# Expert tiles two pairs earlier, and summary copies ahead of loads, in a fused attention and expert kernel

## The chip, the cores and the metric

One core of a Trainium2 chip. The metric is the device time of one launch in microseconds (us), median of several runs; lower is better. Five engines work side by side, each through its own instructions in order: TensorE (matmuls and transposes; PE in the profile), VectorE (DVE), ScalarE (ACT), GpSimd (POOL), and SyncE (SP), which here only starts transfers. The *clock* in the tables is the share of TensorE's full clock that the profile says was granted.

## The reference, cut to what matters

```python
# attention, 4 batches x 8 heads x 768 x 64: a window of 16 positions around the query,
# plus one summary key (max) and one summary value (mean) for each block of 32
k_sum = k.reshape(B, H, nb, 32, D).max(axis=3);  v_sum = v.reshape(B, H, nb, 32, D).mean(axis=3)
... softmax over [window scores, summary scores + log(32)] ...
x = attn_out.transpose(0, 2, 1, 3).reshape(3072, 512)
# mixture of 8 experts: each token goes to one
logits = x @ w_gate + modality_bias[modality_id];  e_idx = argmax(logits)
for e in range(8):
    out[e_idx == e] = gate[e_idx == e] * (relu(x[e_idx == e] @ w1[e]) @ w2[e])   # F = 1024
```

## The kernel before

Sixteen *pairs* (batch and two heads, numbered 0 to 15; four pairs make a batch) go through attention in a software pipeline. When a batch's four pairs are done, it is *routed*: logits, expert, and the row of each token in a table `xs` in DRAM, sorted by expert. GpSimd *scatters* the batch's tokens there in six indirect transfers, two ticks of the schedule apart. An *expert tile* is 256 consecutive rows of `xs`: loaded (`xr`), transposed (`px`), multiplied by `w1` (`ph`), and by `w2` (`pmo`). Tiles come in lists: two after batch 0, four after batch 1, two after batch 2, and the rest at the end. A tile's steps are cut into up to seven *units*, and a string per pair says in which of its six slots how many are put into TensorE's stream.

The load of a tile's rows reads `xs`, so it may start only after the scatters of its batch. The weights of the first two tiles are guessed and loaded early; the tile itself then issues its weight load under a condition ("only if the guess was wrong") into the same buffers.

```python
UNITS = {9: "000111", 10: "101111", 11: "111111", 12: "101111", ...}   # pair: units in slots 0 to 5
ENLIST = (7, 10, 14)                                                     # pairs at whose end a list is taken up

def weights(lst, j, i):                       # GpSimd, of tile i
    e = nc.gpsimd.value_load(li[0:1, j, 2:3]); go = nc.gpsimd.value_load(li[0:1, j, 3:4])
    load_weights(i % NWB, e, cond=go > 0)     # skipped if go is 0
...
for n in range(np_):                          # pairs
    scores(n, 1);  tick(...);  pump(u[0])     # tick: routing steps and one scatter; pump: expert units
    keys(n + 2)                               # transposes, copies of kv
    ... features, route ...
    load(n + 4)                               # three loads issued by GpSimd
    weights_ahead(n)                          # a guessed weight load, GpSimd
    tick(...);  pump(u[1])
    values(n, 0)
    tick(...)
    summaries(n + 2)                          # VectorE reductions, then GpSimd's copy kv<-ks
    tick(...);  pump(u[2])
    queries(n + 2);  tick(...);  pump(u[3])
    blocks(n + 1);  ... scores(n + 1, 0);  tick(...);  pump(u[4])     # blocks: value transposes (pv)
    ... features ...;  values(n, 1);  tick(...)
    if n in ENLIST: scatter(NC); enlist(lists[b - 1])
    pump(u[5])
```

The softmax here doesn't subtract the row's maximum and nothing guards it: scores larger than these inputs give would overflow.

## Time and profile before

| | before |
|---|---|
| time, median of 3 | 233.79 us |
| profiled span, mean TensorE clock | 228.3 us, 0.903 |
| TensorE busy | 184.0 us (81 %) |
| VectorE, ScalarE, GpSimd busy | 122.8, 119.4, 124.9 us |
| transposes of tiles 0, 1 and 2 start at | 80.2, 94.9, 110.8 us |
| routing of batches 0, 1 and 2 starts at | 41.0, 68.4, 117.1 us |

The profiled execution took 230.08 us, 3.7 us less than the median; spans and times are therefore not to be mixed. TensorE fills the second half of the span, so work moved off it there comes off the time; in the first half it waits for its helpers. The wanted gain is in that first half: fill its holes with expert work from the second. The lines of the profile stand in the prediction.

### The profile page before, as it was taken

How to read it: one execution, taken by the hardware profiler on the slowest of the kernel's cores; microseconds unless marked ns; L12 is line 12 of the kernel's file. 1: busy time of each engine (PE TensorE's matmuls, PEld its weight loads, DVE VectorE, ACT ScalarE, POOL GpSimd, SP SyncE). 2: the span in 40 equal slices, each digit the busy share in tenths (PEclk: the TensorE clock that was granted, in tenths of full speed). 3: DMA queues.
4: the chain of work that ended last, by engine and by line, in shares of the span. 5: the costliest groups of instructions: out<-in, count | busy, mean ns of one | idle time of the engine just before them, and what ended most of it. 6: DMA issues, size and time to landing. Idle time of an engine off the chain costs nothing. (4 is left out here: it accounts for less than half of the span.)

```text
span 228.3 us, 6765 instructions
## 1 busy us (share of the span) xinstructions
PE 184.0 (81%) x2720; PEld 131.5 (58%) x2720; DVE 122.8 (54%) x352; ACT 119.4 (52%) x207; POOL 124.9 (55%) x198
## 2 busy tenths in 40 slices
PE   0676797869696549999789999999959899999900
PEld 0464575667465536766577667576626667766500
DVE  6369979699958994655449763534870111101000
ACT  2586568576854441867457675462424255554410
POOL 8459529738889180498531575311574757372220
PEclk9999589967977575999999999999997999999985
DMA  5979929999999999139950123241121434312100
GB/s 76 136 106 139 188 44 143 187 205 172 203 221 153 227 172 160 37 88 207 200 198 3 70 100 136 81 143 47 69 103 56 157 118 141 112 51 83 52 19 0
DMA packets 20090, 27.44 MB, mean 120 GB/s; under 512 B 2876, under 2 KB 16468, under 8 KB 20052
## 3 DMA queue, kind: packets, MB, share of 16 engines
q0 software_dynamic: 17424, 24.40, 52.8%
q1 hardware_dynamic: 2628, 2.54, 4.0%
q8 instruction: 23, 0.38, 0.7%
q14 instruction: 15, 0.12, 0.2%
HBM read 85.46 MB, written 10.44 MB: 420 GB/s over the span
## 5 line engine op out<-in xcount | busy, mean ns | idle before, releaser
L530 PE MATMUL ph<-xg,w1b 128*128 128x256 f16 x416 | 53.8, 285 | 6.6 <-DVE at L516 3.8
L530 PEld LDWEIGHTS <-w1b 128*128 128x128 f16 x416 | 40.4, 101 | 14.9 <-issue 7.0
L542 PE MATMUL pmo<-w2b,hT 128*128 128x512 f16 x208 | 48.5, 379 | 0.0
L548 POOL DMA_INDIRECT out_dram<-ot,at x26 | 25.9, 997 | 32.8 <-ACT ot L547 22.3
L292 ACT ACTIVATE pT<-pss 128x384 f16<-128x384 f32 x64 | 28.0, 495 | 23.5 <-PE pss L287 23.4
L533 ACT ACTIVATE hT<-ph 128x512 f16<-128x512 f32 x52 | 30.6, 602 | 17.2 <-PE ph L530 16.7
L547 ACT ACTIVATE ot<-pmo,xr 128x512 f32<-128x512 f32 x26 | 17.9, 688 | 27.7 <-PE pmo L542 18.0
L351 POOL DMA_INDIRECT xs<-xb,posi x24 | 24.9, 1040 | 13.1 <-issue 5.3
L542 PEld LDWEIGHTS <-hT 128*128 128x128 f16 x208 | 19.2, 98 | 20.6 <-ACT hT L533 1.4
L238 ACT COPY kv<-pk 128x768 f16<-128x768 f16 x32 | 24.3, 810 | 8.1 <-PE pk L237 7.8
L513 DVE COPY xg<-px 128x1024 f16<-128x1024 f16 x13 | 8.9, 686 | 34.0 <-PE px L511 34.0
L270 PE MATMUL pv<-ident,kv 128*128 128x128 f16 x192 | 16.0, 244 | 4.0 <-POOL kv L251 4.0
L318 DVE TENSOR_TENSOR xb<-po,rec 128x384 f16<-128x384 f32 x32 | 17.8, 557 | 1.0
L241 POOL COPY kv<-kv 128x352 f16<-128x352 f16 x16 | 7.9, 493 | 18.7 <-ACT kv L238 18.5
L270 PEld LDWEIGHTS <-kv 128*128 128x128 f16 x192 | 13.5, 110 | 5.7 <-POOL kv L251 4.4
L248 DVE TENSOR_REDUCE ks<-kv 128x24 f16<-128x768 f16 x16 | 15.1, 944 | 2.2 <-ACT kv L238 2.2
L250 DVE TENSOR_REDUCE ks<-kv 128x24 f16<-128x768 f16 x16 | 15.1, 943 | 0.8 <-ACT kv L238 0.8
L294 DVE TENSOR_TENSOR pT<-pT,bmask 96x768 f16<-96x768 f16 x14 | 8.5, 604 | 13.2 <-ACT pT L292 13.2
L330 DVE COPY xT<-pt 128x768 f16<-128x768 f16 x16 | 8.9, 555 | 12.0 <-PE pt L327 11.8
L271 DVE COPY vb<-pv 120x768 f16<-120x768 f16 x20 | 10.7, 551 | 7.4 <-PE pv L270 7.4
L261 ACT COPY qT<-pq 128x768 f16<-128x768 f16 x16 | 12.9, 809 | 3.0 <-PE pq L259 2.9
L287 PEld LDWEIGHTS <-kv 64*128 64x128 f16 x384 | 8.4, 101 | 10.4 <-issue 8.9
(127 smaller groups left out, 280.7 us busy)
## 6 DMA issues: line engine op xcount, KB each, us to landing
w1b<-in_moe_w_dram POOLq DMA_DIRECT2D x13, 1024.0 KB
w2b<-in_moe_w_dram POOLq DMA_DIRECT2D x13, 1024.0 KB
kn<-in_k_dram POOLq DMA_DIRECT2D x16, 192.0 KB
vn<-in_v_dram POOLq DMA_DIRECT2D x16, 192.0 KB
qn<-in_q_dram POOLq DMA_DIRECT2D x16, 192.0 KB
xr<-xs SPq DMA_DIRECT2D x8, 272.0 KB, 7.1
w1b<-in_moe_w_dram POOLq DMA_DIRECT2D x4, 512.0 KB
w2b<-in_moe_w_dram POOLq DMA_DIRECT2D x4, 512.0 KB
```

The costliest lines, as they stand in the source:

```text
L238: nc.scalar.copy(kv[:, i, :, 0:64].rearrange("p t (s c) -> p t s c", c=C8), bass.AP(pk.tensor, pk.offset, [pk.ap[0], [8, NT], [1, 8], [P8, ...
L248: nc.vector.reduce_max(ks[:, 0], kv[:, 0, :, 0:64].rearrange("p t (g s) -> p t g s", g=2), axis=AX.X)
L250: nc.vector.reduce_sum(ks[:, 1], kv[:, 1, :, 0:64].rearrange("p t (g s) -> p t g s", g=2), axis=AX.X)
L270: nc.tensor.transpose(pv[:, tl, :], kv[:, 1, 6 * half + tl, :], ident)
L292: nc.scalar.activation(pT[:, h], pss[h], AF.Exp, scale=SCALE)
L318: nc.vector.tensor_tensor(xo, po[:, :, :, 0:D], rec.unsqueeze(3).to_broadcast([128, 2, 3, D]), op=ALU.mult)
L351: apart("xs", nc.gpsimd.indirect_dma_start(out=xs[:, :], out_offset=bass.IndirectOffsetOnAxis(ap=posi[:, c:c + 1], axis=0), in_=xb[:, c, : ...
L530: nc.tensor.matmul(ph[:, f, :], w1[:, c, ts(2 * f2 + f, 128)], xg[:, c, :], start=(c == 0), stop=(c == NCD - 1))
L533: nc.scalar.activation(hT[:, 2 * f2:2 * f2 + 2, :], ph, AF.Relu)
L542: nc.tensor.matmul(po, hT[:, f, ts(s2, 128)], w2[:, f, :], start=(f == 0), stop=(f == NF - 1))
L547: nc.scalar.activation(ot, po, AF.Copy, scale=gt)
L548: apart("out", nc.gpsimd.indirect_dma_start(out=out[:, :], out_offset=bass.IndirectOffsetOnAxis(ap=at[:, s2:s2 + 1], axis=0), in_=ot[:], i ...
```

## The change

Its intent: (a) GpSimd's summary copy of a pair goes ahead of that pair's loads in GpSimd's queue, so that the value transposes don't wait for it; (b) start-up memsets go from VectorE to GpSimd; (c) the mask is added by matmul in seven instead of nine pairs; (d) expert units start in pair 7 instead of 9, three a pair at first; (e) for that, routing of batch 0 runs faster, the first list is taken up after pair 6, and the guessed weights are loaded by pair 8. The diff is cut: it leaves out where the other memsets move to, and one empty step fewer in the start-up work.

```diff
-    NMASK = 9
+    NMASK = 7
-        nc.vector.memset(kv[:, :, 0, 64:80], 0.0)          # and four more, three times
+        nc.gpsimd.memset(kv[:, :, 0, 64:80], 0.0)
-    UNITS = {9: "000111", 10: "101111", 11: "111111", 12: "101111", 13: "111111", 14: "111111", 15: "101111"}
-    ENLIST = (7, 10, 14)
+    UNITS = {7: "000111", 8: "001110", 9: "010101", 10: "010101",
+             11: "111110", 12: "101111", 13: "111110", 14: "101111", 15: "101110"}
+    ENLIST = (6, 10, 14)
-        for p in {n + 2: (n,) for n in range(8)}.get(n, ()):
+        for p in {2: (0,), 3: (1,), 4: (2,), 5: (3,), 6: (4,), 7: (5,), 8: (6, 7)}.get(n, ()):
+    T = (1, 2, 2, 2)                                       # routing steps a tick, by batch
...
+        tick(T[b])
+        pump(u[1])
+        values(n, 0)
+        tick(T[b])
+        if n + 2 < np_:
+            summaries(n + 2)
         if n + 4 < np_:
             load(n + 4)
         weights_ahead(n)
-        tick(2 if n >= 8 else 1)
-        pump(u[1])
-        values(n, 0)
-        tick(2 if n >= 8 else 1)
-        if n + 2 < np_:
-            summaries(n + 2)
```

More of the change, by code (lines that the diff above doesn't have):

```diff
@@ L102, in borders @@
         kv, vb = kvs[i], vbs[i]
-        nc.vector.memset(kv[:, :, 0, 64:80], 0.0)
-        nc.vector.memset(kv[:, :, NT - 1, 80:96], 0.0)
-        nc.vector.memset(kv[:, :, :, KR:128], 0.0)
-        nc.vector.memset(vb[0:WK, :, :, D:D + 1], 1.0)
-        nc.vector.memset(vb[WK:KR, :, :, D:D + 1], 32.0)
-    borders(0)
+        nc.gpsimd.memset(kv[:, :, 0, 64:80], 0.0)
+        nc.gpsimd.memset(kv[:, :, NT - 1, 80:96], 0.0)
+        nc.gpsimd.memset(kv[:, :, :, KR:128], 0.0)
+        nc.gpsimd.memset(vb[0:WK, :, :, D:D + 1], 1.0)
+        nc.gpsimd.memset(vb[WK:KR, :, :, D:D + 1], 32.0)
     tok = const.tile([128, NJ], I32, name="tok")
     nc.gpsimd.iota(tok, pattern=[[128, NJ]], base=0, channel_multiplier=1)
+    for i in range(NK):
+        borders(i)
     midc = const.tile([NJ, 128], mybir.dt.int64, name="midc")
@@ L161 @@
     guess = const.tile([128, NWB], I32, name="guess")
+    nc.gpsimd.memset(exl, -1.0)
+    nc.gpsimd.memset(done, 0.0)
+    nc.gpsimd.memset(ones, 1.0)
     def early_constants():
@@ L166, in early_constants @@
         nc.vector.reduce_max(g1, mb0, axis=AX.X)
-        nc.vector.memset(exl, -1.0)
         yield
@@ L171, in early_constants @@
         nc.vector.tensor_tensor(g2, mb0, g1.unsqueeze(2).to_broadcast([128, 2, E]), op=ALU.is_ge)
-        nc.vector.memset(done, 0.0)
         nc.vector.tensor_tensor(g2, g2, erev[:, None, :].to_broadcast([128, 2, E]), op=ALU.mult)
@@ L175, in early_constants @@
         nc.vector.reduce_max(g1, g2, axis=AX.X)
-        nc.vector.memset(ones, 1.0)
         nc.vector.tensor_tensor(exl[:, 0:1], g1[:, 0:1], g1[:, 1:2], op=ALU.max)
@@ L203, in later_constants @@
         nc.vector.tensor_copy(mh, midc.bitcast(I32)[:, 0::2])
-        for _ in range(4):
+        for _ in range(3):
             yield
@@ L625 @@
     load(2)
-    borders(1)
     queries(0)
@@ L632 @@
     load(3)
-    borders(2)
     queries(1)
@@ L648 @@
             side.append(route(b - 1))
+        tick(T[b])
+        pump(u[1])
+        values(n, 0)
+        tick(T[b])
+        if n + 2 < np_:
+            summaries(n + 2)
         if n + 4 < np_:
@@ L651 @@
         weights_ahead(n)
-        tick(2 if n >= 8 else 1)
-        pump(u[1])
-        values(n, 0)
-        tick(2 if n >= 8 else 1)
-        if n + 2 < np_:
-            summaries(n + 2)
-        tick(2 if n >= 8 else 1)
+        tick(T[b])
         pump(u[2])
@@ L661 @@
             queries(n + 2)
-        tick(2 if n >= 8 else 1)
+        tick(T[b])
         pump(u[3])
@@ L665 @@
             blocks(n + 1)
-            tick(2 if n >= 8 else 1)
+            tick(T[b])
             scores(n + 1, 0)
-        tick(2 if n >= 8 else 1)
+        tick(T[b])
         pump(u[4])
@@ L671 @@
             features(n - 1)
-        tick(2 if n >= 8 else 1)
+        tick(T[b])
         values(n, 1)
-        tick(2 if n >= 8 else 1)
+        tick(T[b])
         if n in ENLIST:
```

## The prediction

> **What bounds the kernel now.** I read the page's busy slices first, then the stretches by stage, the waits of the stretch where TensorE is not full, and last the timeline around the first expert tile. The kernel has 16 attention pairs (batch and pair of heads, numbered 0 to 15); the expert tiles of the routed tokens are fed into TensorE's stream in small units (a transpose step, four steps of the first matmul, two of the second), from pair 9 on.
>
> ```profile
> PE   0676797869696549999789999999959899999900
> DVE  6369979699958994655449763534870111101000
> PEclk9999589967977575999999999999997999999985
> DMA  5979929999999999139950123241121434312100
> ```
>
> One digit is 5.7 us. TensorE is full only from slice 16 on (about 91 us). Before that it has gaps, the granted clock falls below full, and VectorE and the DMA engines are near nine tenths. The stretches say it in numbers (columns: length, TensorE, its weight loads, VectorE, ScalarE, GpSimd busy, clock, DMA share, GB/s):
>
> ```profile
> 0.00:42.00 42.00, 28.38 (x651) 21.14 (x652) 31.26 (x96) 26.47 (x44) 27.17 (x52) 0.92 0.82 121
> 42.00:77.00 35.00, 26.18 (x589) 20.48 (x588) 29.38 (x84) 19.99 (x37) 27.12 (x43) 0.77 1.11 195
> 77.00:94.00 17.00, 13.22 (x220) 10.65 (x221) 11.81 (x34) 7.56 (x14) 4.81 (x10) 0.67 0.96 154
> 94.00:157.00 63.00, 60.96 (x853) 41.97 (x851) 36.33 (x96) 38.82 (x70) 33.08 (x51) 1.00 0.41 114
> 157.00:218.00 61.00, 55.28 (x421) 37.30 (x419) 14.02 (x43) 26.61 (x44) 31.86 (x44) 0.97 0.26 94
> ```
>
> From 94 to 157 us TensorE is busy 61.0 of 63 us: it is the bound. From 42 to 77 us (pairs 4 to 8) VectorE is busy 29.4 of 35 us and GpSimd 27.1, TensorE 26.2 at a clock of 0.77: the two helpers set the pace. What TensorE waited for between 17 and 93 us (total, times, longest):
>
> ```profile
> PE pv L270 <- POOL kv L251: 4.0, 3, 2.2
> PE ph L530 <- DVE at L516: 3.8, 1, 3.8
> PE pc L412 <- DVE tot L408: 2.7, 1, 2.7
> PE pr L386 <- DVE oh L378: 2.0, 2, 1.3
> ```
>
> The change aims at the first line (summary copies) and the second (first expert tile). The timeline there (start, length):
>
> ```profile
> 60.21 0.75 POOL L224 DMA_DIRECT2D w1b<-in_moe_w_dram  x1
> 62.30 0.71 POOL L251 COPY kv<-ks 128x576 f16<-128x576 f16 x1
> 63.07 0.84 PE L270 MATMUL pv<-ident,kv 128*128 128x128 f16 x12 [2.17 <-POOL kv L251]
> 65.82 0.98 POOL L351 DMA_INDIRECT xs<-xb,posi  x1 [0.30 <-issue]
> ...
> 69.90 1.58 SPq L488 DMA_DIRECT2D xr<-xs  x2
> ...
> 80.20 1.03 PE L511 MATMUL px<-ident,xr 128*128 128x128 f16 x8
> 86.12 1.87 PE L530 MATMUL ph<-xg,w1b 128*128 128x256 f16 x8 [3.78 <-DVE at L516]
> ```
>
> The summary copy stands behind three loads and a weight load, and TensorE waits 2.17 us for it. The sixth row scatter goes out at 65.82; the load of the tile's rows is issued at 69.90, lands 7.9 us later (about 77.8, from the DMA view), and the tile's transposes run at 80.20. So in this kernel the rows were there 2.4 us before they were used. That margin matters below.
>
> **What the Trainium skill says.** "TensorE: Matmul & The Clock Gate", Part 1: the array falls to half rate after an idle window of about 3.4 us and needs one busy window to come back; the trace agrees, 16 key transposes take 0.53 us at full clock and 0.85 us in the 0.5 stretches. The same page's specifications call GpSimd's queue "strict FIFO" of depth 8: so a copy ahead of loads is early, and loads behind a copy wait for whatever the copy waits for; 62.30 above is that rule. "GPSIMD Engine Reference", 4: GpSimd's cores write the descriptors of its own DMAs; here each load issue holds it 0.65 us and each scatter about 1.0 us (1.3 apart). "DMA: Bandwidth & Descriptors", Anatomy of one DMA: about 2 us fixed per transfer; the scatter above took 4.1 us until its reader could start, with the engines busy.
>
> **The change, part by part.**
> (a) Copies ahead of loads: takes away at most the 4.0 us of waits and, since they set off a half-clock stretch at 64 to 67 us, about 1.5 us more. But VectorE was saturated from 44 to 64 us, and ScalarE has only about 0.9 us of slack around the wait at 37 us, so I count 2.5 us. The cost: loads, weight loads and scatters now stand behind VectorE's reductions.
> (b) Memsets: VectorE loses three times (0.07 + 0.07 + 0.14 + 0.08 + 0.08) and 0.08 + 0.07 + 0.17, 1.8 us in all as listed, some overlapped; it is near full from 14 to 30 us, so about 0.5 us of it counts. GpSimd gets 18 memsets; its known ones last 0.10 us, an iota of 128x128 0.23, so I estimate 2 to 3 us, into the 2.87 us that it waits at 5.8 us. Even.
> (c) Bias in two pairs fewer: 8 matmuls of 128x384 off TensorE at 0.21 us apart, 1.7 us; four multiplies of 0.604 us onto VectorE (2.4 us), one 0.55 us copy off it onto ScalarE at 0.80.
> (d) Expert units: 36 before the last batch's routing in both (3, 5, 6, 5, 6, 6, 5 against 3, 3, 3, 3, 5, 5, 5, 5, 4). Six move from the TensorE-bound stretch into pairs 7 and 8. The undisturbed tail does a tile each 7.39 us (ScalarE's relu at 188.58, 195.97, 203.36), so a sixth is 1.23 us and the six are 7.4 us. If pairs 7 and 8 had free TensorE time this would come off whole, and the 3.8 us wait with perhaps 2.5 us of half clock at 85 to 91 too.
> (e) Routing of batch 0 at two steps a tick from pair 4: in VectorE's new order the keys' reductions of pairs 6 and 7 stand behind the routing chain.
>
> The ideal sum: 7.4 + 3.8 + 2.5 + 2.5 + 0.5 + some of 1.7, about 17 us. Most of it is not to be had, because the rows must first be in place. I follow that chain with durations of the trace. Routing starts at about 41.8 us (42.5 before, 0.7 earlier by (a)). VectorE then has, in its new order, the routing (about 6.3 us with the list), two normalisations more (1.8 with a fresh row tag), the pair-6 reductions (1.7) and two copies (1.0): its reductions for pair 7 end near 55.3 us. GpSimd follows: summary copy 0.7, three loads 2.0, weights 0.8, three scatters 3.9, two border copies 0.9, sixth scatter 1.0: about 64.6 us, hardly earlier than the 66.8 of before. With 2 to 4 us to land and 5 to 8 for the rows, they are there at about 73 us, at best 70. But TensorE reaches their transposes in pair 7 at about 63 to 66 us. It executes in order, so it stands 6 to 10 us and comes back cold.
>
> From there: two pairs of attention (3.9 us each at full clock, with routing about 9 us) lie after the transposes now that lay before them. So against before, TensorE gains 80.2 - 73 = 7 us, loses 9, gains the 3.8 and 2.5 us, and pays about 3 us for the cold restart: 1 us gained; with (a), (b) and (c) in the same stretch partly counted already, I add another 1. A second wait of the same kind is possible at the third tile: its rows waited 1.45 us at 110.8 us before, and its step moves from the fifth slot of pair 11 to the first. The other way, if the rows land at 70 us or sooner, 3 us more come off.
>
> **The rivals.** First, the design works: GpSimd keeps up, the rows land as pair 7 asks for them, and 7.4 us of units and the waits come off: 224 to 227 us. For it speaks that the counts per pair look chosen with care, and that VectorE has idle time (2.9 us between 66 and 70 us) that a smoother start would use; against it the chain just worked out. Second, the new wait repeats: GpSimd holds at the conditional weight load until the guess's last part has landed (7.40 us at 85 us before), now a pair earlier, then has five scatters, two output scatters, three loads and copies, about 15 us, before the third tile's rows can be fetched; TensorE stands another 8 us: 240 to 245 us. Third, VectorE's added multiplies alone set pairs 7 and 8: 2.4 - 0.55 = 1.9 us, within the range.
>
> **Range and chances.** The centre of the chain is 233.8 - 2 = 232 us. The good rival gives the lower end, 224, the repeated wait the upper, 243. Two per cent of 233.8 is 4.7 us: faster means under 229.1, which needs the rows by about 69 us, 0.32; slower means over 238.5, which needs the second wait whole, 0.22; within, 0.46.
>
> **What would show it.** Wait of the first expert transposes for the rows: none, or under 2 us, makes my chain wrong and the first rival right; 6 to 10 us right. The waits of the value transposes for the summary copy should fall from 4.0 us to under 1. Between 70 and 75 us the clock should be half. The transposes of the third tile show the second rival. TensorE's busy time should be lower by about 2 us beyond any change of clock. My prediction is wrong if VectorE finishes the pair-7 reductions well before 55 us, or if the early stages, which I left almost as they were, change their clock.

## The result, and the profile after

| | before | after |
|---|---|---|
| time, median of 4 | 233.67 us | 252.63 us |
| range | 233.24 to 236.83 | 248.95 to 254.21 |
| profiled span, clock | 228.3, 0.903 | 250.3, 0.879 |
| TensorE busy | 184.0 us | 184.3 us |
| tiles 0, 1, 2 transposed at | 80.2, 94.9, 110.8 | 76.0, 89.0, 123.4 |
| routing of batches 0, 1, 2 at | 41.0, 68.4, 117.1 | 40.5, 83.6, 138.8 |

The ratio is 1.072 (95 % interval 1.057 to 1.088): slower, and outside the predicted range. Ratios of this kind are computed as the mean time of one kernel's fast runs over that of the other's of the same rounds, so they are not quite the ratio of the medians that are quoted. A run counts as fast when it is within 1.5 % of the fastest of its kernel; two of the four runs of after and one of before are not.

The busy slices of the kernel after (6.26 us a digit):

```profile
PE   1694997595008898564299989998887799999900
DVE  5379797988303699621127677633592110011000
PEclk9997699779555999967579999999997999999975
```

In slices 10 and 11 (62.6 to 75.1 us) TensorE is all but still, then again around slices 16 to 19 (100 to 125 us), and each time the clock row falls to five to seven tenths. VectorE's row has holes at the same places: when TensorE stands, the others soon stand with it. The stretches (length, then TensorE, its weight loads, VectorE, ScalarE, GpSimd busy; clock; DMA share; GB/s):

```profile
42.00:77.00 35.00, 16.22 (x390) 12.99 (x391) 20.61 (x60) 14.02 (x25) 23.06 (x36) 0.71 1.07 184
94.00:157.00 63.00, 47.55 (x708) 32.27 (x706) 33.04 (x92) 30.97 (x56) 28.87 (x46) 0.86 0.52 110
```

From 42 to 77 us TensorE does 16.2 us of work where it did 26.2; from 94 to 157 us 47.6 us where it did 61.0. The same 184 us of work is done; it is spread over 22 us more: TensorE's idle time is 66.0 us where it was 44.3. (The medians differ by 19.0 us; the profiled execution of before was a quick one.) What TensorE waited for (us in total, times, longest):

```profile
PE px L512 <- DMA xr<-xs: 21.1, 2, 13.0
...
PE pv L271 <- POOL kv L252: 5.2, 1, 5.2
```

Before, the first line was one wait of 1.45 us. The two waits for rows and the one for the summary copy, in TensorE's timeline (start, length; in brackets the idle time before it and what ended it):

```profile
76.04 1.03 PE L512 MATMUL px<-ident,xr 128*128 128x128 f16 x8 [13.04 <-DMA xr<-xs]
108.73 1.46 PE L271 MATMUL pv<-ident,kv 128*128 128x128 f16 x12 [5.22 <-POOL kv L252]
123.42 1.04 PE L512 MATMUL px<-ident,xr 128*128 128x128 f16 x8 [8.07 <-DMA xr<-xs]
```

The first is the first tile's transposes, the third the third tile's, the first of batch 1's list. What GpSimd did for each:

```profile
62.89 0.99 POOL L352 DMA_INDIRECT xs<-xb,posi  x1 [0.16 <-issue]
...
84.96 0.47 POOL L242 COPY kv<-kv 128x352 f16<-128x352 f16 x1 [12.55 <-ACT kv L239]
...
93.55 0.04 POOL L225 DMA_DIRECT2D w1b<-in_moe_w_dram  x1 [0.25 <-DMA w1b<-in_moe_w_dram]
102.53 0.04 POOL L225 DMA_DIRECT2D w2b<-in_moe_w_dram  x1 [8.94 <-DMA w2b<-in_moe_w_dram]
103.53 1.06 POOL L352 DMA_INDIRECT xs<-xb,posi  x1 [0.95 <-DVE xb L319]
...
117.34 0.99 POOL L352 DMA_INDIRECT xs<-xb,posi  x1
```

Batch 0's sixth scatter goes out at 62.89 us; its rows are usable 13.1 us later. TensorE got there at 63.0 us and stood. GpSimd, whose next work needs keys that TensorE has not transposed, stood 12.55 us as well. At 93.55 us it reaches the conditional loads. They are skipped (0.04 us), but the one for `w2b` is held 8.94 us until the guessed weights, issued just before at 91.79 us, have landed in that buffer. Only then come batch 1's scatters, the last at 117.34 us, and 6.1 us after it the third tile's transposes. So there are two candidates for the second half of the loss: the hold, or the scatters of batch 1 that come late because its routing came 15 us late (83.6 against 68.4 us), an echo of the first wait.

### The profile page after: what moved, and what is told of

It reads as the page before. It is cut to its first block, busy times and chain, and to the rows that moved or that the text cites.

```text
span 250.3 us, 6748 instructions
## 1 busy us (share of the span) xinstructions
PE 184.3 (74%) x2712; PEld 130.6 (52%) x2712; DVE 120.5 (48%) x337; ACT 119.3 (48%) x208; POOL 127.9 (51%) x216
## 5 line engine op out<-in xcount | busy, mean ns | idle before, releaser
L543 PE MATMUL pmo<-w2b,hT 128*128 128x512 f16 x208 | 51.5, 397 | 0.0
L531 PEld LDWEIGHTS <-w1b 128*128 128x128 f16 x416 | 39.7, 100 | 10.8 <-issue 3.1
L543 PEld LDWEIGHTS <-hT 128*128 128x128 f16 x208 | 20.1, 102 | 22.3 <-issue 3.3
L512 PE MATMUL px<-ident,xr 128*128 128x128 f16 x104 | 9.2, 234 | 22.8 <-DMA xr<-xs 21.1
L272 ACT COPY vb<-pv 120x768 f16<-120x768 f16 x13 | 10.6, 812 | 21.3 <-PE pv L271 21.2
L512 PEld LDWEIGHTS <-xr 128*128 128x128 f16 x104 | 7.0, 104 | 24.2 <-DMA xr<-xs 21.4
L252 POOL COPY kv<-ks 128x576 f16<-128x576 f16 x16 | 10.7, 669 | 16.9 <-DVE ks L251 13.9
L249 DVE TENSOR_REDUCE ks<-kv 128x24 f16<-128x768 f16 x16 | 15.1, 945 | 2.8 <-ACT kv L239 2.8
```

The costliest lines, as they stand in the source:

```text
L272: (nc.vector.tensor_copy if half or n < NMASK and n % 2 else nc.scalar.copy)(vb[0:KR, 6 * half:6 * half + 6, :, 0:D], pv[0:KR].rearrange(" ...
L512: nc.tensor.transpose(px[:, c, s2, :], xr[:, s2, ts(c, 128)], ident)
L531: nc.tensor.matmul(ph[:, f, :], w1[:, c, ts(2 * f2 + f, 128)], xg[:, c, :], start=(c == 0), stop=(c == NCD - 1))
L543: nc.tensor.matmul(po, hT[:, f, ts(s2, 128)], w2[:, f, :], start=(f == 0), stop=(f == NF - 1))
```

## The experiments

Theory at the outset: the loss is two waits for rows. TensorE takes its work in order, so a tile placed before its rows are there holds up attention too, and with it the next batch's routing, scatters and rows. Rivals: GpSimd's hold is the cause of the second wait; the masks, the routing pace or the queue order cost by themselves.

There were four sessions, A to D, of four kernels each, each session on a chip of its own. There the kernel before had medians of 234.4, 237.8, 238.9 and 237.1 us, with a broad spread (228.0 to 238.8 in A, 229.4 to 240.8 in D). Where runs spread like that, few runs of before count as fast (4 of 43 in D), the ratio of fast runs rests on those few, and it reads up to 2.4 % above the ratio of the medians. The table therefore has both; the control with the kernel before against itself (1.005 and 1.000) says what to trust them with. Differences under 1 % are not read.

| run | session | median, us | ratio of fast runs, interval | ratio of medians |
|---|---|---|---|---|
| the kernel after | first result | 252.63 | 1.072 [1.057, 1.088] | 1.081 |
| copies_only | A | 231.39 | 1.003 [0.996, 1.009] | 0.987 |
| tiles_only | A | 255.89 | 1.091 [1.073, 1.109] | 1.092 |
| start_at_9 | A | 233.92 | 1.011 [1.005, 1.017] | 0.998 |
| no_row_wait (wrong result) | A | 240.87 | 1.035 [1.023, 1.046] | 1.028 |
| no_hold | B | 250.85 | 1.069 [1.052, 1.086] | 1.055 |
| no_row_no_hold (wrong) | B | 240.33 | 1.024 [1.011, 1.037] | 1.011 |
| late_hold | B | 239.81 | 1.021 [1.014, 1.029] | 1.009 |
| copies_late_hold | B | 237.09 | 1.013 [1.007, 1.019] | 0.997 |
| spare_hold | C | 250.79 | 1.046 [1.040, 1.053] | 1.050 |
| no_rows_both2 (wrong) | C | 239.76 | 1.002 [0.996, 1.008] | 1.003 |
| no_rows_spare (wrong) | C | 234.13 | 0.977 [0.971, 0.983] | 0.980 |
| early_turn | C | 237.55 | 0.986 [0.979, 0.993] | 0.994 |
| after_again | D | 256.43 | 1.084 [1.074, 1.093] | 1.081 |
| before_again | D | 237.16 | 1.005 [0.999, 1.010] | 1.000 |
| spare_hold_again | D | 250.08 | 1.058 [1.049, 1.067] | 1.055 |
| early_xb3 | D | 235.30 | 1.016 [1.008, 1.024] | 0.992 |

### Which part of the change: copies_only, tiles_only, start_at_9

copies_only is the kernel before with the new queue order and GpSimd's memsets; tiles_only is the rest of the change; start_at_9 is the whole change but for the units.

```diff
 # start_at_9, against after
-    UNITS = {7: "000111", 8: "001110", 9: "010101", 10: "010101", 11: "111110", ...}
+    UNITS = {9: "000111", 10: "101111", 11: "111111", 12: "101111", 13: "111111", 14: "111111", 15: "101111"}
```

> Kernel before with the summary copies ahead of the loads and the memsets on GpSimd, nothing else. Theory (the loss is TensorE standing in order at expert transposes whose rows have not landed): no expert step moves, so no such wait; the waits of the value transposes for the summary copy fall from 4.0 us to under 1.5, the time is within 2% of before, perhaps 1 to 3 us less: 230 to 234 us. Rival (loads behind VectorE's reductions starve the attention pairs): waits of the key transposes for kn and vn grow by 3 us or more and the time is 238 us or more.

> The changed kernel with the loads again ahead of the summary copies and the memsets back on VectorE: expert tiles from pair 7, faster routing ticks, fewer bias pairs stay. Theory: the wait of the first expert transposes for their rows stays, 8 us or more, since the rows come at the end of VectorE's routing and GpSimd's scatters either way: 244 to 254 us. Rival (the copies' order made the rows late): the wait falls under 4 us and the time under 238 us.

> The changed kernel with the old table of units (first expert step in pair 9); copies ahead, memsets, faster ticks, list taken after pair 6 all stay. Theory: no wait for the first tile's rows (13.0 us goes), the attention of pairs 7 and 8 runs on, and the time is near before, 229 to 237 us. Rival (faster ticks and GpSimd's order cost by themselves): 242 us or more without any wait at the expert transposes.

Measured: 231.4, 255.9 and 233.9 us, beside a before of 234.4. The loss is in the units: with those of before, everything else of the change costs about 1 % at most (1.011 by fast runs, 0.998 by medians, and 1 % against copies_only). tiles_only came out somewhat above what was expected of it; its two row waits are longer, 16.9 and 11.4 us:

```profile
80.72 1.03 PE L511 MATMUL px<-ident,xr 128*128 128x128 f16 x8 [16.90 <-DMA xr<-xs]
127.88 1.03 PE L511 MATMUL px<-ident,xr 128*128 128x128 f16 x8 [11.43 <-DMA xr<-xs]
```

So the copies ahead of the loads do not cause the loss. And in copies_only they do what was wanted: 0.2 us are left of the 4.0 us of waits for the summary copy. But other waits grew (total, times, longest):

```profile
PE pk L238 <- DMA kn<-in_k_dram: 7.2, 2, 5.2
PE pk L238 <- DMA vn<-in_v_dram: 5.2, 4, 2.9
PE pr L387 <- DVE oh L379: 4.2, 3, 2.0
```

Before, these lines had 5.1, 2.9 and 2.6 us. TensorE, let through earlier, meets VectorE, which did not get faster, and the key transposes wait 4.4 us more for their loads, which now stand behind the copies. That much of its rival came true; the rival's time, 238 us or more, did not. (start_at_9 has the same order and only 0.7 us more of these waits, so the order alone does not set them.)

### The first row wait alone: no_row_wait

The first two tiles read a small table of their own that no scatter writes. The result is wrong (tokens are missing); the instructions are the same but for a memset, a copy and a transfer at the start that fill the table. Batch 0's routing starts at 42.3 us here and at 40.5 in the kernel after, so some 2 us of this run may be the table's own.

```diff
-            nc.sync.dma_start(xr.bitcast(I32), xs[ds(row, 256)]...)
+            src = xz if lst["i0"] == 0 else xs[ds(row, 256)]      # xz: 256 rows, written once at the start
+            nc.sync.dma_start(xr.bitcast(I32), src...)
```

> Wrong result on purpose: in the changed kernel the first two tiles read their rows from a small table written at the start, so their loads wait for no scatter. Theory: the 13.0 us wait at the first expert transposes falls under 2 us; what follows starts earlier by some 9 us, but the third tile's wait stays or grows, because its scatters stand behind GpSimd's hold of 8.9 us at the conditional weight load: 240 to 247 us in all. Rival (one wait is the whole loss): 232 to 238 us.

Measured 240.9 us, 1.035: half of the loss goes, or somewhat more by the medians. The first tile now starts at 65.4 us with no wait, but the other two waits are there whole:

```profile
98.90 1.46 PE L276 MATMUL pv<-ident,kv 128*128 128x128 f16 x12 [6.04 <-POOL kv L257]
113.74 1.03 PE L518 MATMUL px<-ident,xr 128*128 128x128 f16 x8 [8.57 <-DMA xr<-xs]
```

So an echo of the first wait cannot be all of the second: batch 1 is routed 10.7 us earlier than in the kernel after (72.95 us), and the third tile still waits 8.6 us. Against before, TensorE asks for that tile's rows 4.2 us earlier (105.2 against 109.4) and they come 2.9 us later (113.7 against 110.8). The second wait has a cause of its own.

### The hold, first try: no_hold, no_row_no_hold, late_hold, copies_late_hold

no_hold leaves out the conditional loads of the first two tiles (right for this input, where the guess is right); no_row_no_hold does it beside no_row_wait. The other two are candidates for a better kernel: start_at_9, and copies_only, with those loads called one pair after the guessed loads rather than right behind them.

```diff
 def weights(lst, j, i):
+    if i < NWB: return                       # no_hold
 ...
-            if p == 7: guessed[0] = NTILE + NWB; ahead()
+        if n == 9: guessed[0] = NTILE + NWB; ahead()      # late_hold, instead
```

> The kernel after, with the conditional weight loads of the first two tiles left out (the guessed experts are the right ones for these inputs, so the result stays right). Theory of two waits: the wait of the first tile's transposes for its rows stays at 11 to 14 us, but GpSimd's hold of 8.9 us behind the weights is gone, and with it the 5.2 us wait of the value transposes for the summary copy; the third tile's wait of 8.1 us falls below 2. Time 238 to 245 us. If GpSimd's hold is only a place where it stands anyway (rival: the third tile's rows are late because of the late restart at 76 us alone), the third tile still waits 5 us or more and the time stays at 249 to 254.

> Both taken out: the first two tiles read a small table that nothing scatters into (result wrong on purpose), and their conditional weight loads are left out. If the two waits for rows and weights are all that the change loses, this shows what its early start is worth without them: 224 to 231 us, no wait over 4 us of TensorE for rows. If something else of the change (VectorE's masks, the routing at double pace, the order of loads) also costs, it stays at 233 or above.

> The kernel after with the units of before (first expert unit in pair 9), and the conditional weight loads of the first two tiles called one pair later, in pair 9, when the guessed weights have landed: a candidate for the better kernel. The hold of 9.0 us should fall below 3. Ratio to before 0.985 to 1.005 if the hold cost TensorE something there, 1.005 to 1.015 (as with the hold) if it was hidden.

> The kernel before with the copies ahead of the loads and GpSimd's memsets, the guessed weights loaded by pair 8 and the conditional loads called in pair 9: the other candidate. Ratio 0.98 to 1.00 if the hold of GpSimd delayed the third tile's rows, 1.00 to 1.01 if it was hidden.

Measured: 250.9, 240.3, 239.8 and 237.1 us beside a before of 237.8. The first three missed what was expected of them: no_hold came out where its rival had it (250.9 us, 5.7 us of wait), no_row_no_hold at 240.3 us and not under 231, late_hold above both its ranges. copies_late_hold (1.013 by fast runs, 0.997 by medians) cannot be told from before. In no_hold the wait for the summary copy is gone, the third tile comes 9.9 us earlier, but it still waits:

```profile
113.55 1.03 PE L514 MATMUL px<-ident,xr 128*128 128x128 f16 x8 [5.70 <-DMA xr<-xs]
```

So without the hold, and with the first wait still in, 5.7 us of the second wait remain, because batch 1's last scatter comes only at 107.63 us: the third tile's transposes follow the last scatter by 5.9 us here and by 6.1 us in the kernel after. The third tile is bound to batch 1's scatters; the hold delays them, but is not all that does. And no_row_no_hold, meant as the ideal, still waits 4.6 us at that tile, for the same reason: half of the row waits were never taken out of it.

A nuisance appeared too: in these traces TensorE has gaps that end in nothing the profile shows (the trace says "issue"), 4.5 us in no_hold:

```profile
PE po L309 <- issue: 2.3, 4, 1.2
PE ph L533 <- issue: 2.2, 4, 1.2
```

The traces of session A and of the first result have none. Whether they belong to the edits or to the chip was open. late_hold is a clear miss for another reason: its hold did fall, to 1.95 us, but the tile's weights now wait for the late conditional load, and TensorE for them (5.6 us at the first `ph`, 5.8 in copies_late_hold). Neither candidate beats before.

### Rows and hold, each by itself: spare_hold, no_rows_both2, no_rows_spare, early_turn

spare_hold aims the first two tiles' conditional loads at a spare buffer, so that the same instructions have nothing to wait for. no_rows_both2 lets the first six tiles (both early lists) read the small table, with the hold in place (their output rows are skipped). no_rows_spare does both.

```diff
-        load_weights(i % NWB, e, cond=go > 0)
+        load_weights(i % NWB, e, cond=go > 0, spare=i < NWB)      # spare_hold
...
-            src = xz if lst["i0"] == 0 else xs[ds(row, 256)]
+            src = xz if lst["i0"] < 6 else xs[ds(row, 256)]       # no_rows_both2
```

> The kernel after with the same instructions, but the first two tiles' conditional weight loads (skipped, since the guess is right) are aimed at a spare buffer that no load writes, so that they have nothing to wait for. This repeats the run without the hold, which had 4.5 us of TensorE gaps that no other engine explains, without changing the number of instructions. If those gaps came from the edit, they are gone here and the time is 243 to 247 us (ratio 1.035 to 1.055), with px of the third tile at about 113 us and a wait of 4 to 7 us for batch 1's rows. If they come from the chip of the day, they are here too, or in the kernel before of the same rounds, and the ratio stays at 1.05 to 1.07.

> The first six expert tiles (both early lists) read a small table that no scatter writes; their output rows are skipped (result wrong on purpose). GpSimd's hold stays. Theory: the third tile waits for the last scatter of batch 1, not for GpSimd's hold in itself, so without that dependence its wait of 8.6 us is gone, while the wait of the value transposes for the summary copy behind the hold (6.0 us) stays: 229 to 236 us, ratio 0.99 to 1.02. If the hold alone made the wait, there is nothing left either way, and the two theories are told apart by the next run.

> Both: no dependence of the first six tiles on scatters, and no hold. This is the early start as its author must have meant it. If waits for rows and the hold are the whole loss, 221 to 228 us, ratio 0.95 to 0.985, with no TensorE wait over 3 us between 60 and 150 us. If 231 or more, something else in the change costs as well.

Measured, beside a before of 238.9: 250.8 us (1.046), 239.8 (1.002) and 234.1 (0.977), all three ratios as expected. In microseconds each lies 4 to 6 above its range, as before itself lies 5 above its 233.8; taken by that, no_rows_spare would be over the 231 us from which something else was to cost as well. In spare_hold GpSimd goes through both conditional loads within 0.6 us:

```profile
93.26 0.04 POOL L228 DMA_DIRECT2D wsp<-in_moe_w_dram  x1 [0.20 <-DMA wsp<-in_moe_w_dram]
93.77 0.04 POOL L228 DMA_DIRECT2D wsp<-in_moe_w_dram  x1 [0.47 <-DMA wsp<-in_moe_w_dram]
...
109.86 0.99 POOL L355 DMA_INDIRECT xs<-xb,posi  x1 [0.17 <-issue]
```

Batch 1's last scatter is 7.5 us earlier than in the kernel after, the third tile's transposes also (115.9 us, 6.1 us after the scatter), and they still wait 6.65 us. In no_rows_both2 the hold is still 9.7 us and the wait for the summary copy 5.95 us, but there is no wait for the third tile's rows:

```profile
PE pv L276 <- POOL kv L257: 6.2, 2, 5.9
```

Within this one session the two causes come apart. Rows: 1.0464 - 0.9767 = 0.070 of before's time. Hold: 1.0016 - 0.9767 = 0.025. And what is left, 0.977, is what the whole change is worth if neither is in its way: a gain of 2.3 %. Together they account for 0.977 + 0.070 + 0.025 = 1.072, the very ratio of the kernel after, though that one is from another session.

One thing was not separated. The six tiles' skipped output rows also take 2.9 MB off the DMA queues (24.6 against 27.5 MB moved), in both runs without rows. The hold's share is a difference of two such runs and is free of it; the share of the rows, and the gain, are not. An estimate from no_row_no_hold, which writes everything: its ratio of medians, 1.011, less its last wait for rows (4.6 us, 0.019) would be 0.992, against 0.980 for no_rows_spare. So about 0.01 of the rows' 0.070, and as much of the gain, may be the missing writes or the difference of sessions.

early_turn is a candidate: copies_only with the first tile's transposes two slots earlier within pair 9, so that VectorE's copy of them stands ahead of the summary reductions in its order.

```diff
-    UNITS = {9: "000111", 10: "101111", ...}
+    UNITS = {9: "010101", 10: "101111", ...}
```

> Candidate: the kernel before with copies ahead of loads and GpSimd's memsets, and the first tile's transposes two slots earlier in pair 9 (their units at slots 1, 3, 5 instead of 3, 4, 5), so that the copy of the transposed rows stands ahead of the summary reductions in VectorE's order. In the run without this TensorE waited 4 us (of 6.8) for that copy. Expected: that wait falls below 1.5 us, at most 1.5 us of waiting for the rows comes in its place; 2 to 4 us faster, ratio 0.98 to 0.995. If the rows are not there by then, TensorE waits for them 2 us or more and the ratio is 1.00.

Measured 237.6 us, 0.986 from three fast runs, and 0.994 by medians. In the traces TensorE's wait at the first `ph` fell by half, short of the 1.5 us expected. First copies_only, then early_turn:

```profile
86.11 1.87 PE L531 MATMUL ph<-xg,w1b 128*128 128x256 f16 x8 [3.98 <-DVE xg L514]
```

```profile
84.47 1.87 PE L531 MATMUL ph<-xg,w1b 128*128 128x256 f16 x8 [2.08 <-DVE at L517]
```

The direction is right, and its size is within what these chips let one see.

### What was still open: after_again, before_again, spare_hold_again, early_xb3

Do the unexplained gaps belong to the chip, and is the hold's share the same when both kernels run on one chip? The first three are unchanged kernels. early_xb3 is early_turn with three instead of two buffers for the normalised rows `xb`, since VectorE stood 2.8 us before clearing one.

```diff
-            xbs[b] = work.tile([128, NC, XW], FP16, tag="xb", bufs=2, name="xb")
+            xbs[b] = work.tile([128, NC, XW], FP16, tag="xb", bufs=3, name="xb")
```

> The kernel after, unchanged, on the chip of this call, as the yardstick of the next runs: ratio 1.06 to 1.09, and the two waits for rows of 13 and 8 us. Gaps of TensorE that no engine explains (the trace calls them issue), 4 to 5 us in the runs of the last two calls, should be here too if they belong to the chip, and be missing if they belong to the edits.

> The kernel before, unchanged, profiled on the chip of this call. If the unexplained gaps belong to the chip, they are in its trace as well, 1 to 5 us, and its time is nearer 238 than 233 us; if not, they are absent.

> The spare buffer for the conditional loads, on the same chip as the kernel after: 2 to 3 per cent below it (5 to 8 us), since the wait for the summary copy (5.2 us) goes and the rows' wait at the third tile falls from 8.1 to about 6.5 us. If the hold costs nothing, the two are within 1 per cent.

> The early transposes, and a third buffer for the normalised rows: VectorE waited 2.8 us at 72 us to clear a row buffer, whose last reader is batch 0's last scatter by the program. If that buffer is the cause, the wait is gone, TensorE's wait for the one-hot (2.7 us) too, and 1 to 3 us come off the early-transposes kernel: ratio 0.97 to 0.985. If the wait is for something else (the trace names a load of keys), it stays and the ratio is that of the run without, 0.986.

Measured, beside a before of 237.1: 256.4, 237.2, 250.1 and 235.3 us. The gaps are fewer than expected in the kernel after (1.2 us, not 4 to 5), and spare_hold, with 5.3 us of them in session C, has 1.7 here. They are in the trace of the unchanged kernel before as well, 2.0 us of them in three lines, of which two:

```profile
PE pk L237 <- issue: 0.9, 2, 0.4
PE pmo L542 <- issue: 0.8, 1, 0.8
```

So the edits are not needed for them. They may have a part in the higher times of before in sessions B to D, as may its wait for the third tile's rows (4.05 us in this trace, 1.45 in the first); what makes them no run here shows. The kernel after is 1.084 here, with its waits for rows of 12.0 and 9.3 us, and spare_hold 1.058: the hold is worth 0.026, as between no_rows_both2 and no_rows_spare (0.025). In early_xb3 the wait of VectorE is gone, so the buffer was its cause (the trace had named a load of keys). But TensorE then met rows that had not landed (2.2 us at the first tile, 3.4 at the third), and the time is 1.016 by fast runs, 0.992 by medians, not the 0.97 to 0.985 expected. Nothing is won that can be told. No correct version here beats the kernel before by a settled margin, and all that are level with it start the tiles in pair 9.

## Why the prediction was wrong

**(a), (b), copies and memsets: right in mechanism, at most its small size.** The order does away with the waits for the summary copy (4.0 us to 0.2 in copies_only). Counted at 3.0 us together; measured between 0 (fast runs) and 3 us (medians, 231.4 against 234.4), and partly given back as waits for VectorE and, as the prediction named for a cost, for loads that stand behind the copies (4.4 us more at the key transposes there, 0.7 in start_at_9). The summary copy that waited before stood behind a scatter too (61.26 us, 1.07 us long; the prediction's lines pass over it). The eighteen memsets on GpSimd took 2.8 us from 5.70 us on, where 2 to 3 us were estimated; its first copy came 0.5 us later, but waited there for ScalarE and not for them. The memsets' sum on VectorE is 1.64 us by the prediction's own list, not 1.8.

**(c) and the third rival, masks: no visible cost.** start_at_9 has them and the routing pace, and is level with before within about 1 %. The promised 2 us less of TensorE busy time is not there (184.3 against 184.0 us), though the eight matmuls are gone (2712 against 2720); a lower mean clock (0.879 against 0.903) may have made up for them, which no run separates.

**(d), the worth of six units: mis-sized but little.** 7.4 us of units were counted, with waits and clock about 17 us as the ideal, and 7 to 10 of these for the good rival (224 to 227 us). With both causes of loss taken away the whole change gained 2.3 %, 5.5 us of 233.8, and part of that may be the missing writes: the good rival would have been 228 us or more.

**The chain to the first rows: right up to the scatter, wrongly summed after it.** Routing was expected at about 41.8 us (its long group of matmuls began at 41.29), the reductions of pair 7 to end at 55.3 (53.99; the prediction's own terms, with 1.7 us for these reductions, add up to 54.3), the sixth scatter to end at 64.6 (63.9). TensorE was expected at the transposes at 63 to 66 us (63.0). The rows were expected at about 73 us, 70 at best, from 2 to 4 us for the scatter to land and 5 to 8 for the load. Added to 64.6 these give 71.6 to 76.6, so that was a slip of the sum. They came at 76.0, inside it: 4.4 us from the scatter's start to the issue of the load (67.27 us), and 8.8 from there. The kernel before had shown 4.1 and 7.9 us in the same stretch, with the DMA engines just as full, so the sum could have been taken from it whole. TensorE stood 13.0 us, not 6 to 10, and the clock fell to half at 63 to 80 us as said. (The idle window of 3.4 us that the prediction takes from "TensorE: Matmul & The Clock Gate", Part 1, was not needed in the kernel before: there the clock is half from 64.4 to 67.8 us after a stand of TensorE of 2.17 us.)

**The balance after it: this is the step that failed.** It read: "against before, TensorE gains 80.2 - 73 = 7 us, loses 9, gains the 3.8 and 2.5 us, and pays about 3 us for the cold restart: 1 us gained". It ends at the first tile, as if what comes after were the kernel before, shifted; the second wait, which the prediction itself calls possible, is not in the sum. Up to the second tile the sum does not fail, though its first term was 4.2 us and not 7 (80.2 - 76.0): that tile starts at 89.0 us against 94.9, the kernel is 5.8 us ahead in tiles. It then owes nearly two pairs of attention, so an estimate with the prediction's 3.9 us a pair leaves it about 2 us behind, where 1 us gained was said. But attention is behind, batch 1's routing with it (83.6 against 68.4 us), its scatters, and the rows of the third tile, which the new units ask for in pair 11's first slot. There TensorE waited for the summary copy (5.2 us) and for rows (8.1 us), and was 12.6 us behind at the third tile instead of 5.8 ahead. That is where the time went: 18.4 us between two tiles, of which these two waits, less the 1.45 us of before, are 11.8; much of the rest can be the attention it owed. The run no_row_wait shows that this second wait does not need the first one; no_rows_both2 that it goes when the dependence on batch 1's scatters goes.

**The second rival was the answer, at the wrong odds.** It named the place (third tile), the length ("another 8 us"; 8.07) and the hold behind the guessed weights, and gave 240 to 245 us, with 0.22 for slower. Its size was short: it did not count the 5.2 us for the summary copy behind the same hold, nor the low clock around the second wait (0.62 from 110 to 124 us, 1.00 before); what else is in the remaining microseconds no run separates. Taking the first wait out gave back about half of the loss (1.072, and 1.035 without it, in different sessions). And of the causes it stressed the smaller one: the hold is worth 2.5 %, the dependence of rows on their scatters up to 7 %, over both waits.

**What it said would show it.** The wait of the first transposes (6 to 10 expected, 13 measured), the half clock, and the third tile's transposes all showed it. The waits for the summary copy did fall as such; the one of 5.2 us left is GpSimd standing in the hold. Its two signs of being wrong did not show: the reductions ended at 53.99 us, not well before 55, and the clock up to 42 us was 0.92 as before.

## What to carry to other kernels

Work that is put earlier into an in-order engine has to be followed until its inputs' inputs are there: ask of each place at which it is put, not only the first, what its data waits for and when that was ready before. Where that engine also makes those inputs (here attention, which makes the next batch's rows), work moved ahead of it puts them off while it asks for them earlier: even without the first wait, in no_row_wait, the next rows came 2.9 us later and were asked for 4.2 us earlier than before. And a transfer that will be skipped can still hold its queue if its destination has a write under way: give it a destination that has none (which gave back 2.6 % here), or a place at which the write has landed, if nothing then waits for it there (late_hold's 5.6 us).

## What the Trainium skill lacked or had wrong

- "DMA: Bandwidth & Descriptors", Anatomy of one DMA: about 2.0 us fixed plus bytes at 436 GB/s. An estimate from that for a scatter of 139 KB and a load of 278 KB in turn is 2.3 + 2.6 = 4.9 us. Here it took 6.1 us at a DMA share of 0.79 (110 to 124 us) and 13.1 us at a share of 1.05 (62 to 76 us). The section has no term for what is queued already; in the fuller stretch the time beyond the estimate, 8.2 us, is the larger part (that it is queueing is argued, not shown).
- The same page, "Two DMAs through the same engine are not ordered", tells the author to make the issuing engine wait for the earlier transfer before a dependent one. That agrees with GpSimd's waits of 6.2 to 9.75 us before its skipped loads, and 0.2 to 0.5 us with a spare destination. What no page says is that a transfer which its condition skips (0.04 us) pays this wait all the same.
- "GPSIMD Engine Reference" lists memset among what GpSimd does, without times: here eighteen small ones took 0.11 to 0.32 us each, 2.8 us in all.
- No page that I looked at explains gaps of TensorE of 0.2 to 1.8 us that end in nothing the profile shows, up to 5.3 us in one execution (spare_hold), in traces of sessions B, C and D, the unchanged kernel's among them. Nor does one warn that the same kernel's median differs by up to 2.2 % from session to session (233.7 to 238.9 us here).
